# Batch 1's transposes in one run, one more group of block 2 by quarter products, and key-value products in two other PSUM banks: a fused attention and feed-forward kernel on Trainium2

## The chip, the cores and the metric

The kernel runs on one core of a Trainium2 chip. The metric is the device time of one execution in microseconds. The profile used here is one profiled execution; its engines are TensorE (PE in the profile), VectorE (DVE), ScalarE (ACT), GpSimd (POOL) and SyncE (SP). The differences to be read are a few tenths of a per cent.

## What is computed

For 8 batches and 8 heads, 576 tokens of 64 numbers go through a linear attention without softmax, and its normed rows (8 × 576 = 4608 tokens of 512) through a feed-forward pair with a leaky step between:

```python
kv = np.einsum('bhsd,bhse->bhde', k, v)
out = np.einsum('bhsd,bhde->bhse', q, kv)
rms = np.sqrt(np.mean(out * out, axis=-1, keepdims=True) + 1e-06)
x = (out / rms * g_norm)            # then (4608, 512)
h = x @ w_in                        # 512 -> 2048
g = np.maximum(h, 0.0) + alpha * np.minimum(h, 0.0)
return (g @ w_out).astype(np.float32)
```

## The kernel before

The 4608 tokens are worked in nine **blocks** w = 0 to 8 of 512 tokens. A block's life has these steps, and the names in brackets are those of the order described below.

- **Attention.** k, v and q of a batch are loaded by DMAs that POOL issues (`ld`, behind one-element gate copies that hold a load back until a given result is there, L1478). q is transposed, for batches 0 and 1 on PE by `step_t` (L361, matmuls with an identity into a PSUM tile, then a copy into SBUF), later by DMA transposes on SP (`q`, L405). The key-value products (`kv`, in `kv_runs`, L1407 for batches 3 on) are 72 matmuls of 64×64. ACT copies them to SBUF as `kv_masked` (`kvc`, three copies, L1419 and L1422). The row products (`R`, L575) multiply q with them; ACT squares the rows (`q2`, `q3`, L635, one instruction and one read of the accumulator per head), takes the root (`rs`), DVE scales them (`n`, L661), and SP transposes the result into `xt` by DMA (`x`, L673).
- **First product** (`m1`), x by w_in, in four groups s of 4 × 128 hidden features. A plain group (`M`, L695, or `Ma` with `M` in column pieces, L728) is four matmuls of 128×512 into one PSUM bank; ACT makes the negative part (`r`, L704), DVE the leaky step (`s`, L710) into `gt`. From the block given in `M1_FROM` on, a group goes by **quarter products** instead (`f.w.s.n`, L1296): seven products of quarters, four matmuls of 128×256 each, as in Strassen's scheme, so that 28 matmuls of 256 columns stand for 16 of 512. They need sums of quarters of the weights (`a.s.n`, made once) and of x (`t.w.n`, DVE, L1280 to L1286, made once a block), three ACT copies of partial sums (`seed`, `u2`, `u3`, L1312 and L1315), two DVE sums (`c22`, `c12`, L1318), and per result half a step on ACT (L1356) and on DVE (`s11` and so on, L1363).
- **Second product** (`p`, L948), gt by w_out, also by quarter products with sums (`S`) on DVE; for the first block plain (L740, tiles `y`). Results are put together (`y.w…`) and stored (`st`).

PSUM has eight banks. Three (`h0` to `h2`) serve the first product, two more (`m0`, `m1`, pool `psm`) the first product from block 2 on; the row products and the key-value products share a two-bank tile (`row_tile`, pool `psr2`); one holds the second product.

**What sets the order.** Blocks 0 and 1 are written out in program order. From block 2 on a table `ORDER` of 1085 step names gives the order in which steps are issued, on all engines; each step's function `put_…` lists the steps that it needs. `LATE_KV` = 4: key-value products of batches 4 to 7 are put only after the first two norms of the row tile (`first` in the diff), since they take the row tile's banks, and the second row products of that batch wait for their copies.

Of the kernel before, what the change touches and what calls it, by code (L numbers as in the profile page):

```python
# [17 lines left out]
def kernel(  # L18
# [1833 lines left out]
    for w in range(1, NW):  # L1852
# [9 lines left out]
        ld.q.4.1@s.2.2 S.2.3.0 M.2.8 y.1.u3 ld.v.4.1@- M.2.10 q3.3.1 q3.3.0 p.1.4.0 p.1.4.1 rs.3.1
        p.1.4.2 r.2.8 n.3.1 p.2.1.0 rs.3.0 r.2.10 p.1.4.3 n.3.0 x.3.1 r.2.9 p.2.1.1 S.1.4.0 y.1.c21
        R.3.3 s.2.9 p.2.1.2 q2.3.2 x.3.0 a.1.2 p.1.5.0 S.2.3.1 p.1.5.1 q2.3.3 S.1.4.3 p.2.1.3
        S.1.4.2 q3.3.2 p.1.5.2 s.2.10 p.1.5.3 q3.3.3 M.2.11 a.1.4 s.2.8 rs.3.2 M.2.13 rs.3.3 n.3.2
        r.2.11 y.2.p1 n.3.3 M.2.12 x.3.2 r.2.13 s.2.11 M.2.14 r.2.12 S.2.1.0 ld.v.4.0@s.2.11 x.3.3
        p.2.2.0 y.1.c22 R.4.1 s.2.12 M.2.15 q.4.3 q2.4.0 S.2.2.0 p.2.2.1 r.2.14 s.2.13 p.1.3.0 q.4.2
        r.2.15 p.1.3.1 s.2.14 q3.4.0 p.1.3.2 s.2.15 p.1.3.3 q.4.0 q2.4.1 Ma.3.0 S.2.1.1 M.3.1 q3.4.1
        t.3.1 q.4.1 y.1.c12 ld.q.5.1@! rs.4.0 M.3.0 t.3.3 rs.4.1 M.3.2 y.2.seed n.4.1 st.1.c11 r.3.0
        M.3.3 n.4.0 r.3.2 t.3.2 x.4.0 kv.4 s.3.0 r.3.3 r.3.1 p.2.6.0 S.2.2.1 ld.q.5.4@! kvc.4  # L1870
        f.3.1.1 s.3.2 p.2.6.1 ld.v.5.1@s.2.9 a.3.4 p.2.6.2 f.3.1.seed t.3.4 p.2.6.3 S.2.4.1 f.3.1.6
        y.2.u2 s.3.3 ld.q.4.4@s.2.10 R.4.3 f.3.1.u2 p.2.7.0 s.3.1 q.5.3 q2.4.3 ld.k.5.1@! f.3.1.2
        S.2.4.0 f.3.1.7 f.3.1.r11 f.3.1.5 x.4.1 f.3.1.u3 p.2.7.1 ld.q.5.0@! q3.4.3 p.2.2.2 f.3.1.c22
# [6 lines left out]
        f.3.2.s12 q2.5.1 f.3.3.7 f.3.3.5 S.3.1.0 q.5.0 f.3.3.u3 p.2.5.3 q2.5.0 f.3.3.c22 f.3.3.2  # L1880
        f.3.3.4 y.2.c22 q.4.4 f.3.3.r11 f.3.3.3 f.3.3.r21 S.3.2.0 p.2.3.0 q3.5.0 p.2.3.1 f.3.3.c12
        q.5.2 p.3.1.2 f.3.3.s11 f.3.3.r12 p.2.3.2 f.3.3.r22 p.3.1.3 f.3.3.s12 q.5.4
        ld.q.6.0@f.3.3.s11 Ma.4.0 y.3.p1 f.3.3.s22 p.2.3.3 q3.5.1 st.1.c22 st.1.c12 M.4.0 f.3.3.s21
        M.4.2 r.4.0 st.2.c11 rs.5.0 s.4.0 p.3.2.0 rs.5.1 r.4.2 M.4.1 t.4.1 s.4.2 f.4.1.1 r.4.1 t.4.2
# [118 lines left out]
```

## Time and profile before

| | |
|---|---|
| median of 3 runs | 267.34 us (267.1 to 267.72) |
| profiled execution, its own time | 267.1 us |
| its span | 265.3 us |
| PE matmuls | 2709, busy 259.0 us (98%) |
| DVE, ACT, POOL busy | 234.7 (88%), 200.1 (75%), 84.9 (32%) |
| DMA moved | 35.79 MB, mean 135 GB/s |

The span is the profiled part of the execution; the 1.8 us around it are the start and the end. Busy time is the time that an engine's instructions cover, and a PE that is 98% busy need not be at its best pace: what a matmul costs is read from the distance between starts. In rows of the timeline the columns are start, length (us), engine, line, operation, output<-inputs, shape and count; a bracket is the idle time of that engine ahead of the row, and what ended it.

### The profile page before, as it was taken

Reading aid. Unit: us, or ns where it says so; the run is one execution under the profiler, and the core shown is the slowest. Engines: PE = TensorE matmul, PEld = TensorE weight load, DVE = VectorE, ACT = ScalarE, POOL = GpSimd, SP = SyncE. Lnnn points to the kernel's source line nnn. Section 1 sums busy time; section 2 is a strip of 40 time slices with the busy share of each in tenths; the row PEclk is TensorE's granted clock in tenths of the full one; section 3 lists DMA queues with packets and bytes.
Section 4 is the critical chain, followed back from the end, with each engine's and each line's share of the span. In section 5 each row is a group of like instructions: output and inputs, shape, how many; then the busy total and the mean of one; then the engine's idle time right before and its main releaser. Section 6 shows DMA issues by size and latency. Waiting matters only on the chain.

```text
span 265.3 us, 7216 instructions
## 1 busy us (share of the span) xinstructions
PE 259.0 (98%) x2709; PEld 189.7 (71%) x2709; DVE 234.7 (88%) x474; ACT 200.1 (75%) x707; POOL 84.9 (32%) x147
## 2 busy tenths in 40 slices
PE   5999999999999999999999999999999999999995
PEld 2464454456657568886888688878887888788884
DVE  6459955899886998999999999999999999989993
ACT  2567627777569899998899899979988976778400
POOL 8763552363142219044332180810005000015300
PEclk9999999999999999999999999999999999999999
DMA  7999999998968999999999989897404221104223
GB/s 193 188 201 206 196 197 190 193 194 222 129 92 134 143 133 131 151 153 129 187 141 124 158 157 168 153 212 115 58 20 122 41 42 40 42 0 162 79 81 121
DMA packets 65031, 35.79 MB, mean 135 GB/s; under 512 B 37396, under 2 KB 63012, under 8 KB 64996
## 3 DMA queue, kind: packets, MB, share of 16 engines
q0 software_dynamic: 31792, 24.47, 59.7%
q1 hardware_dynamic: 32500, 10.11, 25.7%
q10 hardware_dynamic: 704, 0.75, 0.9%
q8 instruction: 21, 0.34, 0.6%
q14 instruction: 14, 0.11, 0.2%
HBM read 36.71 MB, written 9.44 MB: 174 GB/s over the span
## 4 chain that ended last, share of the span: by engine, by line
PE 95%; DMA 2%; SPq 1%; ACT 0%; DVE 0%; issue 0%
PE h_ps L695 21%; PE yY L948 16%; PE mY L1296 12%; PE yX L948 11%; PE yZ L948 10%; PE mV L1296 6%; PE y L740 5%; PE mX L1296 3%; PE h_ps L728 2%; PE or_ps L575 2%; DMA y_sb<-in_g_norm_dram 2%; PE kv_ps L1407 1%; PE ssq_ps L500 1%; PE ot_ps L477 1%; PE qt_ps L361 1%; PE h_ps L1105 1%
## 5 line engine op out<-in xcount | busy, mean ns | idle before, releaser
L695 PE MATMUL h_ps<-xt,w_in_sb 128*128 128x512 f16 x252 | 59.6, 379 | 0.0
L710 DVE SCALAR_TENSOR_TENSOR gt<-m_sb,beta_sb,h_ps 128x512 f16<-128x512 f32 x72 | 51.4, 740 | 5.1 <-ACT m_sb L704 4.4
L948 PEld LDWEIGHTS <-s 128*128 128x128 f16 x496 | 47.8, 98 | 7.1 <-DVE s L866 0.5
L704 ACT ACTIVATE m_sb<-h_ps 128x512 f32<-128x512 f32 x72 | 41.7, 607 | 14.1 <-PE h_ps L695 9.1
L752 POOL DMA_DIRECT2D out_dram<-y_sb x37 | 21.6, 591 | 72.0 <-ACT y_sb L1004 38.7
L948 PEld LDWEIGHTS <-gt 128*128 128x128 f16 x384 | 37.3, 98 | 7.4
L635 ACT ACTIVATE sq_sb<-or_ps 128x64 f16<-128x64 f32 x192 | 41.0, 269 | 1.0 <-PE or_ps L575 1.0
L695 PEld LDWEIGHTS <-w_in_sb 128*128 128x128 f16 x252 | 24.2, 98 | 24.4 <-issue 0.3
L635 ACT ACTIVATION_READ_ACCUMULATOR sq_sb<-or_ps 128x1 f32 x192 | 40.3, 254 | 0.0
L948 PE MATMUL yX<-w_out_sb,gt 128*128 128x256 f16 x256 | 37.8, 273 | 0.0
L948 PE MATMUL yY<-wsum,s 128*128 128x256 f16 x256 | 34.4, 273 | 0.0
L1363 DVE SCALAR_TENSOR_TENSOR gt<-m_sb,beta_sb,mh 128x256 f16<-128x256 f32 x72 | 30.9, 477 | 0.6 <-ACT m_sb L1356 0.5
L1318 DVE TENSOR_TENSOR mh<-mV,mu 128x512 f32<-128x512 f32 x36 | 24.7, 687 | 3.3 <-PE mV L1296 1.5
L1356 ACT ACTIVATE m_sb<-mh 128x512 f32<-128x512 f32 x36 | 23.1, 647 | 4.4 <-DVE mh L1318 4.0
L1315 ACT COPY mu<-mY 128x512 f32<-128x512 f32 x36 | 21.6, 599 | 4.5 <-PE mY L1296 4.0
L1296 PEld LDWEIGHTS <-w_in_sb 128*128 128x128 f16 x216 | 20.9, 98 | 3.0
L661 DVE TENSOR_TENSOR x_rows<-or_ps,rstd_r 128x512 f16<-128x512 f32 x27 | 18.1, 683 | 3.0 <-ACT rstd_r L645 2.9
L948 PE MATMUL yZ<-wsum,s 128*128 128x256 f16 x120 | 17.2, 273 | 0.0
L948 PE MATMUL yY<-wsum,gt 128*128 128x256 f16 x128 | 16.9, 272 | 0.0
L740 PE MATMUL y<-w_out_sb,gt 128*128 128x512 f16 x64 | 16.3, 380 | 0.0
L212 POOL DMA_DIRECT2D qst<-in_q_dram x12 | 9.5, 791 | 20.1 <-DMA qt_sb<-qst 15.7
L948 PE MATMUL yZ<-w_out_sb,s 128*128 128x256 f16 x120 | 15.9, 273 | 0.0
(161 smaller groups left out, 466.4 us busy)
## 6 DMA issues: line engine op xcount, KB each, us to landing
kst<-in_k_dram POOLq DMA_DIRECT2D x10, 288.0 KB, 6.6
vst<-in_v_dram POOLq DMA_DIRECT2D x10, 288.0 KB, 6.5
qst<-in_q_dram POOLq DMA_DIRECT2D x10, 256.0 KB, 5.1
out_dram<-y_sb POOLq DMA_DIRECT2D x18, 128.0 KB, 4.6
w_out_sb<-in_moe_w_out_dram POOLq DMA_DIRECT2D x8, 256.0 KB, 12.0
out_dram<-y_sb POOLq DMA_DIRECT2D x7, 256.0 KB, 5.1
out_dram<-y_sb SPq DMA_DIRECT2D x5, 256.0 KB, 2.3
w_in_sb<-in_moe_w_in_dram POOLq DMA_DIRECT2D x2, 512.0 KB, 10.0
```

The costliest lines, as they stand in the source:

```text
L635: nc.scalar.activation(out=sq[:, half, j], in_=o_ps[:, half, j], func=AF.Square, accum_out=ssq[:, half, j : j + 1],)
L695: nc.tensor.matmul(out=h_ps[:], lhsT=w_in_blk(c, g), rhs=xts[w][:, c, :], start=(c == 0), stop=(c == NC - 1),)
L704: nc.scalar.activation(out=neg[w, g][:], in_=h_ps[:], func=AF.Relu, scale=-1.0)
L710: nc.vector.scalar_tensor_tensor(out=gts[w, i][:, r, :], in0=neg.pop((w, g))[:], scalar=beta_sb[:, g : g + 1], in1=h_ps[:], op0=ALU.mult, ...
L740: nc.tensor.matmul(out=y[:], lhsT=gt_cols(w, g, a * P, (a + 1) * P), rhs=w_out_blk(g), start=(n == 1), stop=(n == NF),)
L752: engs[store_turn[0] % len(engs)].dma_start(out=dst, in_=src)
L948: nc.tensor.matmul(out=bank, lhsT=lhs, rhs=rhs, start=fresh, stop=(c == NK - 1), skip_group_check=True,)
L1296: nc.tensor.matmul(out=t[bank][:, r, :], lhsT=lhs[:, c, r * P : (r + 1) * P], rhs=rhs[:, c, :], start=(fresh and c == r == 0), stop=(c == ...
L1315: nc.scalar.copy(out=t[what][:], in_=t["Y"][:])
L1318: nc.vector.tensor_add(out=h_tile(t, what)[:], in0=src[:], in1=u[:])
L1356: nc.scalar.activation(out=dst, in_=h, func=AF.Relu, scale=-1.0)
L1363: nc.vector.scalar_tensor_tensor(out=gts[w, i][:, r, cols], in0=m, scalar=beta_sb[:, g : g + 1], in1=h, op0=ALU.mult, op1=ALU.add,)
```

## The change

Four things are done.

1. The four transposes of batch 1's q on PE are issued in one run, before the second product's matmuls with which they were interleaved, with two of their PSUM tiles from another pool (`O_POOL` in place of `S_POOL` and `Q_POOL`); the second half of batch 1's key-value products also goes to `O_POOL`.
2. `M1_FROM[3]` goes from 3 to 2: group 3 of block 2 is made by quarter products. Four plain groups (`M.2.12` to `M.2.15`) go, `f.2.3.…` and `t.2.1` to `t.2.4` come.
3. Key-value products of batches 4 to 7 go into a tile of two banks of the first product (`m0`, `m1`, taken by a new pool `pskv`). They need the earlier users of these banks instead of the row tile's norms, the first product's next use of the banks needs `kvc`, and the row tile waits only for its own norms.
4. `ORDER` is a new table of 1097 names.

```diff
-    step_t(1, 0, S_POOL)
-    step_t(1, 1, Q_POOL, nc.vector.tensor_copy)
+    step_t(1, 0, O_POOL)
+    step_t(1, 1, O_POOL, nc.vector.tensor_copy)
+    step_t(1, 3, Q_POOL)
+    step_t(1, 2, S_POOL, nc.vector.tensor_copy)
     y_run(3, (8,))
-    step_t(1, 3, O_POOL)
     y_run(0, (9,))
-    step_t(1, 2, S_POOL, nc.vector.tensor_copy)
     y_run(3, (9,))
     step_kv(1, 0, O_POOL)
-    step_kv(1, 1, S_POOL)
+    step_kv(1, 1, O_POOL)
...
-    M1_FROM = {1: 3, 2: 3, 3: 3}
+    M1_FROM = {1: 3, 2: 3, 3: 2}
...
+    def open_m(name):
+        m_ctx.close()
+        m_pool[:] = [m_ctx.enter_context(tc.tile_pool(name=name, bufs=1, space=bass.MemoryType.PSUM)), name]
+
+    def kv_tile(shape, name):
+        open_m("pskv")
+        return m_pool[0].tile(shape, FP32, name=name, tag="kv")
...
     def kv_runs(b):
-        kv_tiles[b] = row_tile([2, H, D], "kv_ps")[:, :, 0 : NPAIR // 2, :]
+        if b >= LATE_KV:
+            kv_ps = kv_tile([P, 2, H, D], "kv_ps")
+        else:
+            kv_ps = row_tile([2, H, D], "kv_ps")
+        kv_tiles[b] = kv_ps[:, :, 0 : NPAIR // 2, :]
...
     def put_m1(w):
+        if LATE_KV <= w + 1 < B:
+            kv_old[w + 1] = bank_free["m0"] + bank_free["m1"]
+            bank_free["m0"] = bank_free["m1"] = (("kvc", w + 1),)
...
-            first = (("n", w, 0), ("n", w, 1)) if w >= LATE_KV else ()
-            step(("kv", w), "kv", lambda: kv_mm(w), (*loaded, *free, *first))
+            step(("kv", w), "kv", lambda: kv_mm(w), (*loaded, *(kv_old[w] if w >= LATE_KV else free)))
...
-            free = (("kvc", w),) if LATE_KV <= w < B else tuple(("n", w, i) for i in tiles)
+            free = tuple(("n", w, i) for i in tiles)
...
-        kv.3 Ma.2.0 kvc.3 S.1.1.3 M.2.3 S.1.1.2 S.1.1.1 y.1.seed M.2.0 a.2.2 M.2.1 S.1.1.0 S.1.2.1
+        y.1.seed kv.3 M.2.1 S.1.1.1 t.2.1 p.1.2.3 r.2.1 M.2.3 S.1.1.2 S.1.1.0 a.1.1 Ma.2.0 r.2.3
```

**Where instructions stand, on PE.** First, batch 1's q in the middle of the second product of block 0. Before (`qst` is q as loaded, `qt_ps` its transpose, `y_…` the output tiles):

```order
L740 MATMUL y_579<-w_out_sb_176,gt 128x512
L361 LDWEIGHTS qst
L361 MATMUL qt_ps<-ident_202,qst 64x128
...
L740 MATMUL y_576<-w_out_sb_176,gt 128x512
L361 LDWEIGHTS qst
...
L740 MATMUL y_577<-w_out_sb_176,gt 128x512
L361 LDWEIGHTS qst
...
L740 MATMUL y_576<-w_out_sb_176,gt 128x512
L458 LDWEIGHTS kst
```

The same place of the changed kernel (L374 is the old L361, L754 the old L740, L471 the old L458):

```order
L754 MATMUL y_579<-w_out_sb_176,gt 128x512
L374 LDWEIGHTS qst
L374 MATMUL qt_ps<-ident_202,qst 64x128
...
L754 MATMUL y_576<-w_out_sb_176,gt 128x512
L754 MATMUL y_577<-w_out_sb_176,gt 128x512
L754 MATMUL y_576<-w_out_sb_176,gt 128x512
L471 LDWEIGHTS kst
```

All 32 transposes now stand together, and the three output matmuls behind them.

Second, the key-value products of batch 4 (`kst`, `vst`). Before, they stand between a plain group of block 3 and the second product of block 2:

```order
L695 MATMUL h_ps<-xt,w_in_sb_166 128x512
L1407 LDWEIGHTS kst
L1407 MATMUL kv_ps<-vst,kst 64x64
L948 LDWEIGHTS s_1621
L948 MATMUL yY<-wsum_624,s_1621 128x256
```

In the changed kernel (L588 is the old L575, L1425 the old L1407, L962 the old L948, L1310 the old L1296):

```order
L588 LDWEIGHTS qt_sb_120
L588 MATMUL or_ps<-kv_masked,qt_sb_120 128x64
L1425 LDWEIGHTS kst
L1425 MATMUL kv_ps<-vst,kst 64x64
L1310 LDWEIGHTS vst
L1310 MATMUL mV<-xt,vst 128x256
```

They moved to directly behind batch 4's first row products, among the quarter products of block 2. Batch 6's have moved likewise behind `R.6.1`; batches 5 and 7 still stand between large matmuls.

Third, what follows batch 5's products in the changed kernel (L742 is the old L728, L709 the old L695):

```order
L1425 MATMUL kv_ps<-vst,kst 64x64
L962 LDWEIGHTS s_1991
L962 MATMUL yZ<-w_out_sb_188,s_1991 128x256
L742 LDWEIGHTS w_in_sb_157
L742 MATMUL h_ps<-xt,w_in_sb_157 128x384
L742 MATMUL h_ps<-xt,w_in_sb_157 128x128
L709 LDWEIGHTS w_in_sb_166
L709 MATMUL h_ps<-xt,w_in_sb_166 128x512
```

Before, batch 5's products stood inside block 4's quarter products; now block 4's first groups follow them, and the 128x512 group in the last row is the first that takes one of the two banks in which the products lie.

More of the change, by code (lines that the diff above doesn't have):

```diff
@@ L73 @@
     m_pool = []
+    m_ctx = ExitStack()
     def late_pools():
@@ L79, in late_pools, with m_tile @@
         ]
-        m_pool.append(
-            ctx.enter_context(tc.tile_pool(name="psm", bufs=1, space=bass.MemoryType.PSUM))
-        )
+        ctx.enter_context(m_ctx)
+        open_m("psm")
+    def open_m(name):
+        m_ctx.close()
+        m_pool[:] = [m_ctx.enter_context(tc.tile_pool(name=name, bufs=1, space=bass.MemoryType.PSUM)), name]
+    def m_tile(shape, name, tag):
+        if m_pool[1] != "psm":
+            open_m("psm")
+        return m_pool[0].tile(shape, FP32, name=name, tag=tag)
+    def kv_tile(shape, name):
+        open_m("pskv")
+        return m_pool[0].tile(shape, FP32, name=name, tag="kv")
     def row_tile(shape, name):
@@ L689, in m1_bank @@
     def m1_bank(tag, shape, name):
-        pool = ps_h if tag[0] == "h" else m_pool[0]
-        return pool.tile(shape, FP32, name=name, tag=tag)
+        if tag[0] == "m":
+            return m_tile(shape, name, tag)
+        return ps_h.tile(shape, FP32, name=name, tag=tag)
     def m1_mm(h_ps, w, g, cs):
@@ L1862 @@
[L1862 to L1873, printed above, removed]
@@ L1880 @@
[L1880 to L1884, printed above, removed]
-        p.3.2.1 y.2.c12 f.4.1.seed M.4.3 s.4.1 y.3.seed f.4.1.6 t.4.4 f.4.1.2 t.4.3 f.4.1.u2 S.3.1.1
@@ new lines @@
+        S.2.3.1 q3.3.2 M.2.11 S.1.4.3 a.1.3 q3.3.3 f.2.3.2 t.2.4 f.2.3.6 y.1.c22 rs.3.2 p.2.1.2
+        r.2.11 n.3.2 f.2.3.5 f.2.3.u2 s.2.11 p.1.3.0 x.3.2 rs.3.3 f.2.3.r11 f.2.3.7 n.3.3 p.2.1.3
+        f.2.3.u3 f.2.3.s11 p.1.3.1 x.3.3 y.2.p1 f.2.3.4 f.2.3.c22 p.1.3.2 ld.q.5.4@f.2.3.s11
+        f.2.3.r21 S.2.1.0 q.4.1 R.4.1 f.2.3.r22 kv.4 f.2.3.s21 q2.4.0 f.2.3.3 S.2.2.0 q.4.0 p.1.3.3
+        kvc.4 p.2.2.0 f.2.3.c12 p.2.2.1 f.2.3.s22 q.4.2 f.2.3.r12 Ma.3.0 q3.4.0 y.1.c12 M.3.0
+        ld.k.5.1@f.2.3.s22 M.3.2 f.2.3.s12 q.4.3 y.2.seed M.3.1 r.3.0 t.3.1 rs.4.0 S.2.1.1
@@ L1955 @@
+        p.8.5.3 p.8.4.0 y.8.c22 p.8.4.1 p.8.4.2 p.8.4.3 p.8.3.0 y.8.c21 p.8.3.1
     """.split()
```

172 lines of the change are left out of this document (93 added, 79 removed).

## The prediction

> **What bounds the kernel now.** I read the busy shares first, then the waits, then stage windows, then single rows of the timeline.
>
> ```profile
> PE 259.0 (98%) x2709; PEld 189.7 (71%) x2709; DVE 234.7 (88%) x474; ACT 200.1 (75%) x707; POOL 84.9 (32%) x147
> PEclk9999999999999999999999999999999999999999
> PE 95%; DMA 2%; SPq 1%; ACT 0%; DVE 0%; issue 0%
> ```
>
> TensorE (PE) is busy for 259.0 of 265.3 us, the granted clock shows no loss in any slice, and 95% of the chain that ended last is PE. The table of PE's waits says what the rest is (total, times, longest):
>
> ```profile
> PE warm_ps L324 <- DVE y_sb L133: 1.5, 1, 1.5
> PE alpha_ps L1069 <- DMA y_sb<-in_g_norm_dram: 0.9, 1, 0.9
> PE qt_ps L361 <- DVE qst L1059: 0.4, 1, 0.4
> ```
>
> All three belong to the start, before any edited code. From there PE runs through, so only two things move the end: PE's own work, and a wait that the new order brings. The windows of blocks 2, 3 and 4 (length, then busy PE, PEld, DVE, ACT, POOL with counts) show how near other engines stand:
>
> ```profile
> 66.60:94.60 28.00, 28.00 (x307) 18.39 (x305) 23.53 (x45) 21.80 (x116) 6.69 (x15) 1.00 0.91 124
> 94.60:120.00 25.40, 25.40 (x310) 20.82 (x309) 24.35 (x50) 24.42 (x106) 10.30 (x19) 1.00 1.13 144
> 120.00:147.70 27.70, 27.70 (x337) 22.93 (x336) 26.54 (x55) 25.34 (x112) 8.86 (x16) 1.00 1.13 142
> ```
>
> PE has no gap; VectorE (DVE) has 4.47 us free in block 2's window and about 1.1 in the two after it.
>
> **Part 1, batch 1's transposes in one go.** PE's timeline before:
>
> ```profile
> 36.10 0.64 PE L361 MATMUL qt_ps<-ident,qst 128*64 128x128 f16 x16
> 36.67 0.39 PE L740 MATMUL y<-w_out_sb,gt 128*128 128x512 f16 x1
> 36.98 0.41 PE L361 MATMUL qt_ps<-ident,qst 128*64 128x128 f16 x8
> 37.33 0.39 PE L740 MATMUL y<-w_out_sb,gt 128*128 128x512 f16 x1
> ...
> 38.32 0.32 PE L458 MATMUL kv_ps<-vst,kst 128*64 128x64 f16 x8
> ```
>
> One output matmul and eight transposes take 37.33 − 36.67 = 0.66 us. Without a change of shape they would take 0.216 (a 512-column matmul, priced below) plus some 0.22 for the transposes (sixteen take 36.67 − 36.10 = 0.57 with one change, so eight take about half of the 0.45 that is left). So one round trip between the shapes costs about 0.225. The stretch from the first transpose to the key-value products is 2.22 us; it holds three trips into the transposes, one of which stays: **−0.45**. The bounds are −0.45 and 0: nothing is gained if the chain behind the transposes (copies of q, then batch 1's rows) is what PE would meet next. The trace has no wait there, so I take −0.45. The copies into SBUF now come in one bunch, with three matmuls and the key-value products as cover.
>
> **Part 2, four groups of block 2 as quarter products.** The pitches come from the chain of waits, which counts runs of equal matmuls:
>
> ```profile
> 85.01 0.87 PE yZ L948 x8
> 87.20 3.45 PE h_ps L695 x16
> ```
>
> A 512-column matmul costs 3.45/16 = 215.7 ns, a 256-column one 0.87/8 = 109 ns. Removed are 16 of the first (3.45 us), added 28 of the second (3.05): **−0.40**. By these rows two halves cost only 2 × 109 − 215.7 = 2.3 ns more than a whole. The Trainium skill ("TensorEngine Tiling (Array Packing)", section "Instruction Overhead") gives every matmul some 60 cycles of overhead, which speaks against cutting matmuls in halves: 16 × (512 + 60) against 28 × (256 + 60) is a saving of 3.3%, 0.11 us instead of 0.40, and the whole sum would be −0.6. The two rows above differ from that by far, and I go by the rows.
>
> What the other engines do for it (count, then busy us and mean ns, from the groups by form):
>
> ```profile
> L710 DVE SCALAR_TENSOR_TENSOR gt<-m_sb,beta_sb,h_ps 128x512 f16<-128x512 f32 x72 | 51.4, 740 | 5.1 <-ACT m_sb L704 4.4
> L1363 DVE SCALAR_TENSOR_TENSOR gt<-m_sb,beta_sb,mh 128x256 f16<-128x256 f32 x72 | 30.9, 477 | 0.6 <-ACT m_sb L1356 0.5
> L1318 DVE TENSOR_TENSOR mh<-mV,mu 128x512 f32<-128x512 f32 x36 | 24.7, 687 | 3.3 <-PE mV L1296 1.5 <-ACT mu L1315 1.2
> L1280 DVE TENSOR_TENSOR t<-xt 128x512 f16<-128x512 f16 x6 | 2.5, 415 | 0.0
> 82.53 1.37 DVE L661 TENSOR_TENSOR x_rows<-or_ps,rstd_r 128x512 f16<-128x512 f32 x2 [2.30 <-ACT rstd_r L645]
> ```
>
> Four sums of x, two of products and eight half-width evacuations come, four full ones go: 4 × 0.415 + 2 × 0.687 + 8 × 0.475 − 4 × 0.740 = +3.9 us of DVE by durations, about 3.1 by start-to-start distance, since neighbours overlap. Block 2's 4.47 free microseconds cover that, so I cost it at **nothing**. The largest piece of that room is the 2.30 in the last row, where DVE waits for ScalarE (ACT) in batch 3's norms. If the new order leaves it idle, 2.2 us of room are left for 3.1 us of work, and PE waits about 0.9. ACT gets some 1.6 us more and has 6.2 free.
>
> **Part 3, key-value products in two banks of the first product.** Two things change on PE. First, where they stand: batches 4 and 6 now come directly behind the row products of the same batch, whose shape is small too. Before, each stood between large matmuls:
>
> ```profile
> 54.23 0.20 PE L1389 MATMUL kv_ps<-vsb,ksb 128*64 128x64 f16 x2
> 54.36 0.29 PE L575 MATMUL or_ps<-kv_masked,qt_sb 64*128 64x64 f16 x8
> ...
> 128.07 0.60 PE L948 MATMUL yX<-w_out_sb,gt 128*128 128x256 f16 x4
> 128.60 0.78 PE L1407 MATMUL kv_ps<-vst,kst 64*64 64x64 f16 x72
> 129.31 0.61 PE L1296 MATMUL mV<-xt,spare 128*128 128x256 f16 x4
> ```
>
> Batch 5's entry costs 0.53 − 4 × 0.109 = 0.09 us beyond the four matmuls. A change between two small shapes (54.23 to 54.36, of which the two products hide little) costs up to 0.12. So a merged pair saves between 0 and 0.21; I take the entry, nearest to what is removed, twice: **−0.19**, with 0 and −0.42 as ends.
>
> Second, the banks: the first product of the next block may use them again only when ACT has copied the products out. Batch 3 shows how long that takes:
>
> ```profile
> 66.78 0.80 PE L1407 MATMUL kv_ps<-vst,kst 64*64 64x64 f16 x72
> 67.52 0.82 PE L728 MATMUL h_ps<-xt,w_in_sb 128*128 128x384 f16 x4
> 67.83 0.37 ACT L1419 CAST kv_masked<-kv_ps 128x256 f16<-128x256 f32 x1 [1.21 <-PE kv_ps L1407]
> 68.21 0.74 ACT L1422 CAST kv_masked<-kv_ps 64x256 f16<-64x256 f32 x2
> ```
>
> The copies end at 68.95, 1.43 us after PE has gone on at 67.52. For batch 5 the new order puts on PE four second-product matmuls (0.44), 4 × 384 columns (0.65) and 4 × 128 (0.22) between the products and the first group in such a bank: 1.30 of cover, so a wait of 0.13; with ACT a little late I take **+0.15**. Queued behind it on PE is all of block 4's first product. Behind batch 7 stand 12 × 0.109 + 4 × 128 columns (0.22) = 1.53, behind batch 4 about 1.75, behind batch 6 far more: nothing. Upper end: ACT comes to the copies a half pass of squares late, which is
>
> ```profile
> 155.19 0.23 ACT L635 ACTIVATE sq_sb<-or_ps 128x64 f16<-128x64 f32 x1
> ...
> 155.97 0.62 ACT L1315 COPY mu<-mY 128x512 f32<-128x512 f32 x1
> ```
>
> 0.78 us for four heads, so up to 0.93 for batch 5. The row tile's second half no longer waits for these copies; PE did not wait there, so that earns nothing.
>
> **Part 4, the loads.** The products move about 6, 9, 10 and 4 us earlier on PE, counted by its work ahead of them. For batch 5 they go from 128.6 to about 119, so its k and v must land by then:
>
> ```profile
> 104.83 9.33 SPq L673 DMA_TRANSPOSE xt<-x_rows  x3
> 112.69 0.18 POOL L1478 COPY gate_sb<-xt 1x1 f16<-1x1 f16 x1 [7.16 <-DMA xt<-x_rows]
> 115.50 0.72 POOL L202 DMA_DIRECT2D vst<-in_v_dram  x1
> vst<-in_v_dram POOLq DMA_DIRECT2D x10, 288.0 KB, 6.5
> ```
>
> Before, GpSimd's (POOL's) last load for it leaves at 115.50, after a gate on transposed x that POOL waited 7.16 us for, and lands 6.5 later, at 122.0. In the new order that gate's transpose is no longer behind batch 4's other half and a transpose of batch 5's q on SP, so I expect the issue near 108 and landing near 115: **nothing**. If the gate stays at 112.7, PE waits 122.0 − 119 = 3 us.
>
> The other steps of the new order trade places within their block: PE's work in them is unchanged, and stores, q's transposes and weight sums keep the same counts on POOL, SP and DVE. I cost them at nothing, under the cover that PE has no row of waiting there now; where that cover fails it is DVE or ACT that is late, which rivals (a) and (c) price.
>
> **The sum.** −0.45 − 0.40 − 0.19 + 0.15 = −0.89. On the profiled execution's own 267.1 us (span 265.3) that gives 266.2; that execution is 0.24 below the median of 267.34, so against the median it is **266.4**. The terms' lower ends together (−0.45, −0.40, −0.42, 0) are −1.27, or 266.1; the largest single step upward, 0.9 us, whether DVE's or a late copy's, gives 267.3. The three runs before lie within 0.3 us of their middle one, and with that on both sides the range is 265.8 to 267.6.
>
> **Rivals.** (a) DVE binds in block 2, as priced: −0.89 + 0.9 = 0, 267.3. For it: the room is in pieces between ACT's results. Against: block 3's window already holds quarter products at 24.35 of 25.40 without a gap of PE. (b) The transposes' gain is lost behind them, 266.4 + 0.45 = 266.85. (c) Slower: ACT reaches the copies late at batches 4, 5 and 7, and PE stops before the first product. With a lag L the waits are L − 0.32, L + 0.13 and L − 0.10; against −1.04 for the rest, the gain is gone at L = 0.44 and a loss of 0.2% stands at L = 0.62. At one half pass of squares, 0.78, they add up to 2.05 and give 267.34 − 1.04 + 2.05 = 268.35. For it: ACT is busy 24.42 of 25.40 us in block 3, and squares stand ahead of the copies of batches 4 and 5. Against: these squares are released by products that PE ends before or during the key-value run. (d) Batch 5's loads stay late: 266.4 + 3 = 269.4. (e) The merges save their upper end and batch 5 has no wait: 267.34 − 1.27 = 266.1.
>
> **How the numbers follow.** Forecast 0.60; (a) 0.11; (b) 0.08; (c) 0.10; (d) 0.04; (e) 0.07. A measurement of this kernel can tell about 0.2%, 0.53 us, from no change: faster is below 266.8. Faster are the forecast and (e): 0.67; same are (a) and most of (b): 0.19; slower are (c) and (d): 0.14. The range 265.8 to 267.6 leaves out (c), (d) and a little of (a).
>
> **What would show it.** In the changed kernel's profile: sixteen output matmuls and transposes in batch 1 without alternation, the stretch near 1.77 us; PE's table of waits still with three rows, or one small row on batch 5's copies; the stretch of the quarter products of block 2 without a gap; key-value products starting within 0.1 us of the row products at batches 4 and 6. A row of PE waiting for ACT's copies, for DVE's sums in block 2, or for k and v would make the prediction wrong, in that order of likelihood; so would DVE gone from its 4.47 us of room to none.

## The result and the profile after

The changed kernel is **slower**: 269.0 us in the median of 20 runs (267.72 to 274.77) against 267.27 for the kernel before (266.95 to 268.42). The ratio is 1.0059, with a 95% interval of 1.0040 to 1.0079. Ratios here leave out executions more than 1.5% above the fastest of their kernel (of the changed kernel's 20 those of 272.43, 272.73 and 274.77), medians do not, and the profiles of e3 and e7 are of such executions. The forecast was 266.4, with a range up to 267.6. The profiled execution took 268.11 us, with a span of 266.3.

The page of the changed kernel, busy shares:

```profile
PE 258.5 (97%) x2721; PEld 191.3 (72%) x2721; DVE 237.3 (89%) x484; ACT 202.6 (76%) x710; POOL 87.8 (33%) x154
```

PE is busy 0.5 us less than before, and the span is 1.0 us longer. The table of PE's waits has a row that the old one lacks (its other two are those of the start):

```profile
PE or_ps L588 <- DMA qt_sb<-qsb: 1.1, 1, 1.1
```

`or_ps` are the row products, `qt_sb<-qsb` the DMA transpose of the rest tokens of a batch's q (q.3.4 in the order). The timeline of SP, before:

```profile
70.14 3.45 SPq L405 DMA_TRANSPOSE qt_sb<-qst  x2
73.77 1.17 SPq L405 DMA_TRANSPOSE qt_sb<-qsb  x1
75.05 2.51 SPq L405 DMA_TRANSPOSE qt_sb<-qst  x2
```

and after:

```profile
70.07 4.76 SPq L418 DMA_TRANSPOSE qt_sb<-qst  x3
74.93 1.20 SPq L418 DMA_TRANSPOSE qt_sb<-qsb  x1
76.22 1.22 SPq L418 DMA_TRANSPOSE qt_sb<-qst  x1
```

The new order puts three transposes of q ahead of q.3.4 in place of two, so it is issued 1.16 us later. The view of that single instruction gives its landing time, before:

```profile
DMA to landing us min/median/max: 2.3/2.3/2.3
```

and after:

```profile
DMA to landing us min/median/max: 3.9/3.9/3.9
```

It landed at 73.77 + 2.3 = 76.1 before and at 74.93 + 3.9 = 78.8 after. It is needed behind the first 8 of the 24 products of batch 3's first rows (R.3.1). PE before, where all 24 run through:

```profile
77.81 0.56 PE L575 MATMUL or_ps<-kv_masked,qt_sb 64*64 64x64 f16 x24
```

and after, where PE reaches them 0.3 us earlier:

```profile
77.48 0.31 PE L588 MATMUL or_ps<-kv_masked,qt_sb 64*64 64x64 f16 x8
78.84 0.54 PE L588 MATMUL or_ps<-kv_masked,qt_sb 64*64 64x64 f16 x16 [1.05 <-DMA qt_sb<-qsb]
```

The eight products ahead take some 0.12, so the sixteen were due at 77.9 before. So 1.9 us of slack, which no view of before had named because nothing waited there, became a wait. The place on SP is not the whole of it: had q.3.4 landed in 2.3 us again, it would have been there at 77.2. e16, the same kernel in a later profile, has it in the same place, and there it lands at 76.3 (2.3 us) and nothing waits. What goes with it is how soon POOL's load of batch 4's q follows it. After, and in e16:

```profile
75.33 0.76 POOL L225 DMA_DIRECT2D qst<-in_q_dram  x1 [3.89 <-DMA qt_sb<-qst]
```

```profile
74.02 1.20 SPq L418 DMA_TRANSPOSE qt_sb<-qsb  x1
...
75.05 0.76 POOL L225 DMA_DIRECT2D qst<-in_q_dram  x1 [3.34 <-DMA qt_sb<-qst]
```

The load is issued 0.40 us behind q.3.4 in the first and 1.03 behind it in e16. All profiles that give q.3.4's landing fall in line: 2.3 us in the eight with the load 0.9 us or more behind it (before, e4, e12 to e14, e16 to e18), 3.7 to 4.4 in the seven with 0.4 to 0.6 (after, e2, e5, e9 to e11, e15), and 6.1 in e3, where the load stands 1.0 ahead of it. No run moves this load alone, so it is a regularity of the profiles and not a shown cause.

The other places, each with its row. Batch 1's transposes:

```profile
36.25 1.08 PE L374 MATMUL qt_ps<-ident,qst 128*64 128x128 f16 x32
37.27 0.82 PE L754 MATMUL y<-w_out_sb,gt 128*128 128x512 f16 x3
38.02 0.32 PE L471 MATMUL kv_ps<-vst,kst 128*64 128x64 f16 x8
```

38.02 − 36.25 = 1.77 us, as forecast. The merged key-value products of batch 4, and those of batch 5 with what follows:

```profile
92.92 0.41 PE L588 MATMUL or_ps<-kv_masked,qt_sb 64*128 64x64 f16 x16
93.26 0.90 PE L1425 MATMUL kv_ps<-vst,kst 64*64 64x64 f16 x72
94.09 0.61 PE L1310 MATMUL mV<-xt,vst 128*128 128x256 f16 x4
...
120.42 0.89 PE L1425 MATMUL kv_ps<-vst,kst 64*64 64x64 f16 x72
121.24 0.61 PE L962 MATMUL yZ<-w_out_sb,s 128*128 128x256 f16 x4
121.69 1.04 PE L742 MATMUL h_ps<-xt,w_in_sb 128*128 128x384 f16 x8
122.56 0.59 PE L709 MATMUL h_ps<-xt,w_in_sb 128*128 128x512 f16 x2
```

No wait for the copies behind batch 5 (121.69 to 122.56 is 0.65 + 0.22 for eight column pieces), none for its loads, and none on DVE in block 2. And the last matmuls, before and after (the spans are 265.3 and 266.3):

```profile
260.95 1.06 PE L943 MATMUL yZ<-w_out_sb,s 128*128 128x128 f16 x16
```

```profile
261.33 1.06 PE L957 MATMUL yZ<-w_out_sb,s 128*128 128x128 f16 x16
```

From that row to the end of the span it is 4.4 us before and 5.0 after. This is the whole account of the 1.0 us. With batch 3's key-value products as a mark (66.78 before, 66.44 after): the first transpose comes 0.15 later; from it to the mark it is 30.68 before and 30.19 after, −0.49; from the mark to the last matmuls 194.17 and 194.89, +0.72; the end +0.6. The +0.72 hold the stop at R.3.1 (1.24 us: the sixteen products start 1.36 after the eight ahead of them, whose own time is some 0.12), so everything else in that stretch is 0.5 **shorter**.

### The profile page after: what moved, and what is told of

It reads as the page before. It is cut to its first block, busy times and chain, and to the rows that moved or that the text cites. A ratio compares the mean times of both kernels' runs of the same rounds, so it can differ in the third digit from the quotient of the medians.

```text
span 266.3 us, 7277 instructions
## 1 busy us (share of the span) xinstructions
PE 258.5 (97%) x2721; PEld 191.3 (72%) x2721; DVE 237.3 (89%) x484; ACT 202.6 (76%) x710; POOL 87.8 (33%) x154
## 4 chain that ended last, share of the span: by engine, by line
PE 94%; DMA 3%; SPq 1%; ACT 0%; DVE 0%; issue 0%
PE h_ps L709 19%; PE yY L962 15%; PE mY L1310 13%; PE yX L962 11%; PE yZ L962 10%; PE mV L1310 6%; PE y L754 5%; PE mX L1310 3%; PE h_ps L742 2%; PE or_ps L588 2%; DMA y_sb<-in_g_norm_dram 2%; PE kv_ps L1425 1%; DMA qt_sb<-qsb 1%; PE ssq_ps L513 1%; PE ot_ps L490 1%; PE qt_ps L374 1%
## 5 line engine op out<-in xcount | busy, mean ns | idle before, releaser
L709 PE MATMUL h_ps<-xt,w_in_sb 128*128 128x512 f16 x236 | 56.8, 379 | 0.0
L962 PEld LDWEIGHTS <-s 128*128 128x128 f16 x496 | 48.1, 98 | 7.3 <-DVE s L880 0.2
L724 DVE SCALAR_TENSOR_TENSOR gt<-m_sb,beta_sb,h_ps 128x512 f16<-128x512 f32 x68 | 48.8, 742 | 4.5 <-ACT m_sb L718 3.7
L718 ACT ACTIVATE m_sb<-h_ps 128x512 f32<-128x512 f32 x68 | 39.8, 608 | 11.3 <-PE h_ps L709 8.5
L962 PEld LDWEIGHTS <-gt 128*128 128x128 f16 x384 | 37.3, 98 | 7.2
L709 PEld LDWEIGHTS <-w_in_sb 128*128 128x128 f16 x236 | 22.4, 98 | 21.7 <-issue 0.3
L962 PE MATMUL yX<-w_out_sb,gt 128*128 128x256 f16 x256 | 36.6, 273 | 0.0
L962 PE MATMUL yY<-wsum,s 128*128 128x256 f16 x256 | 34.3, 273 | 0.0
L1377 DVE SCALAR_TENSOR_TENSOR gt<-m_sb,beta_sb,mh 128x256 f16<-128x256 f32 x76 | 32.9, 478 | 0.6 <-ACT m_sb L1370 0.6
L1370 ACT ACTIVATE m_sb<-mh 128x512 f32<-128x512 f32 x38 | 24.8, 652 | 5.2 <-DVE mh L1332 5.1
L1332 DVE TENSOR_TENSOR mh<-mV,mu 128x512 f32<-128x512 f32 x38 | 26.0, 685 | 1.8 <-ACT mu L1329 1.2
L1329 ACT COPY mu<-mY 128x512 f32<-128x512 f32 x38 | 23.0, 604 | 4.8 <-PE mY L1310 4.5
L1496 POOL COPY gate_sb<-gt 1x1 f16<-1x1 f16 x21 | 7.0, 332 | 54.0 <-DVE gt L1377 38.5
L1310 PEld LDWEIGHTS <-w_in_sb 128*128 128x128 f16 x228 | 22.1, 98 | 3.3
L1377 DVE SCALAR_TENSOR_TENSOR gt<-m_sb,beta_sb,mY 128x256 f16<-128x256 f32 x38 | 16.4, 473 | 0.2
L1377 DVE SCALAR_TENSOR_TENSOR gt<-m_sb,beta_sb,mX 128x256 f16<-128x256 f32 x38 | 16.4, 473 | 0.0
L962 PE MATMUL yZ<-wsum,s 128*128 128x256 f16 x120 | 16.1, 273 | 0.0
L962 PE MATMUL yZ<-w_out_sb,s 128*128 128x256 f16 x120 | 16.1, 273 | 0.0
```

Of the source, the lines that this page charges most:

```text
L709: nc.tensor.matmul(out=h_ps[:], lhsT=w_in_blk(c, g), rhs=xts[w][:, c, :], start=(c == 0), stop=(c == NC - 1),)
L718: nc.scalar.activation(out=neg[w, g][:], in_=h_ps[:], func=AF.Relu, scale=-1.0)
L724: nc.vector.scalar_tensor_tensor(out=gts[w, i][:, r, :], in0=neg.pop((w, g))[:], scalar=beta_sb[:, g : g + 1], in1=h_ps[:], op0=ALU.mult, ...
L962: nc.tensor.matmul(out=bank, lhsT=lhs, rhs=rhs, start=fresh, stop=(c == NK - 1), skip_group_check=True,)
L1310: nc.tensor.matmul(out=t[bank][:, r, :], lhsT=lhs[:, c, r * P : (r + 1) * P], rhs=rhs[:, c, :], start=(fresh and c == r == 0), stop=(c == ...
L1329: nc.scalar.copy(out=t[what][:], in_=t["Y"][:])
```

## The experiments

**e1 to e4, one chip: is it the place of q.3.4 on SP?** e1 is the changed kernel with one swap, e2 the changed kernel again, e3 the kernel before with the same swap the other way, e4 the kernel before with part 1 alone (its diff is the first piece of the change).

```diff
 # e1, in ORDER of the changed kernel
-        p.1.6.0 r.2.5 S.1.2.2 p.1.6.1 q.3.2 y.1.c11 t.2.2 M.2.6 a.1.2 s.2.0 p.1.6.2 q.3.4
+        p.1.6.0 r.2.5 S.1.2.2 p.1.6.1 q.3.4 y.1.c11 t.2.2 M.2.6 a.1.2 s.2.0 p.1.6.2 q.3.2
 # e3, in ORDER of the kernel before: q.3.4 and q.3.2 change places
-        s.2.2 p.1.6.2 p.1.6.3 s.2.0 q.3.4 M.2.6 s.2.1 M.2.4 r.2.6 q.3.3 ld.q.4.0@s.2.2 y.1.u2 s.2.6
+        s.2.2 p.1.6.2 p.1.6.3 s.2.0 q.3.2 M.2.6 s.2.1 M.2.4 r.2.6 q.3.3 ld.q.4.0@s.2.2 y.1.u2 s.2.6
```

> The changed kernel with one swap in the order: the transpose of batch 3's rest tokens (q.3.4) goes to SP third, as before, and q.3.2 fourth. Theory A (the loss is one wait: batch 3's first row products wait for q.3.4, which stands behind one more transpose on SP): the row of PE waiting for qt_sb from qsb, 1.1 us, is gone, the other three rows stay, the span falls by about 1.1, and the median lies near the forecast, 266.3 to 267.0, with a spread as small as that of the kernel before. Rival B (the loss of the median over the profiled run, and its spread of several microseconds, come from another place, such as batch 5's loads or the copies of the key-value products): the row goes, but the median stays above 267.5 and the spread stays.

> The changed kernel once more, unedited, for a second profile. Theory A: the same single new row of PE waiting for qt_sb from qsb, between 0.5 and 4 us, and the time of the profiled run over 267.0 equals it within 0.3. Rival B: a second new row, or a time that this row does not account for.

> The kernel before with the same swap the other way: q.3.4 goes to SP behind all four other transposes of batch 3's q, in place of third. Theory A: it is issued near 76.2 in place of 73.8, lands 2.3 to 3.9 us later, at 78.5 to 80.1, and the first row products need it at 77.9, so PE gets a row of 0.6 to 2.2 us and the kernel is slower by that: 267.9 to 269.5. Rival B (the landing is set by the load and the DMA engines, not by the place in SP's queue): no change, 267.3.

> The kernel before with part 1 of the change alone, batch 1's transposes in one run. Prediction's step: 0.45 us less, 266.85, ratio 0.9983. Rival (the chain behind the transposes takes it back, or it only moves block 2's wait): 267.3.

e3 is the plain one. PE's timeline there:

```profile
77.81 0.31 PE L575 MATMUL or_ps<-kv_masked,qt_sb 64*64 64x64 f16 x8
82.64 0.75 PE L575 MATMUL or_ps<-kv_masked,qt_sb 64*64 64x64 f16 x16 [4.52 <-DMA qt_sb<-qsb]
```

The swap alone costs the kernel before 1.5% (ratio 1.0152, 1.0095 to 1.0208; median 273.06). So the place in SP's queue is enough to bring the wait, which was twice the upper end of what theory A expected. The chain of e3's profile shows why it was so long:

```profile
76.46 6.14 DMA qt_sb<-qsb
```

The later issue alone, with a landing of 2.3, would have made PE wait until 78.8; the other 3.8 us are the longer landing. A long stop also costs more than itself. Stretches of e3's profile behind it (the third number from the end is the granted clock of TensorE, 1.00 in all of these stretches before):

```profile
84.00:86.00 2.00, 2.00 (x7) 0.84 (x6) 0.00 (x0) 2.00 (x19) 0.00 (x0) 0.50 1.32 201
88.00:90.00 2.00, 2.00 (x20) 1.72 (x18) 1.82 (x4) 1.30 (x4) 0.00 (x0) 1.00 0.31 62
```

The granted clock is 0.50 from 82 to 86 us and 0.78 from 86 to 88, and the twelve 512-column matmuls there take 3.90 us in place of 12 × 0.2157 = 2.59. From the mark to the last matmuls e3 takes 200.87, 6.70 more than before: 4.7 of stop and 2.0 behind it. e7 has the same behind its stop of 3.5 us (clock 0.56 and 0.59 in the four us from 72). Behind the stops of 1.1 to 1.8 us in the changed kernel, e1 and e15 the clock stays at 1.00.

e1 removed the wait at R.3.1 as expected, but not the loss (1.0004, 0.9974 to 1.0034; 267.97 in the median). Its lowest time, 266.23, is just the forecast on the profiled run, and its highest 270.96. The unedited kernel on the same chip (e2) is no slower (1.0007), so the ratios cannot tell what the swap is worth. e1's profiled execution took 269.39, with these rows:

```profile
84.03 0.35 PE L588 MATMUL or_ps<-kv_masked,qt_sb 64*128 64x64 f16 x12
84.86 0.23 PE L588 MATMUL or_ps<-kv_masked,qt_sb 64*128 64x64 f16 x4 [0.47 <-DMA qt_sb<-qst]
...
102.52 0.35 PE L588 MATMUL or_ps<-kv_masked,qt_sb 64*128 64x64 f16 x12
104.45 0.23 PE L588 MATMUL or_ps<-kv_masked,qt_sb 64*128 64x64 f16 x4 [1.58 <-DMA qt_sb<-qst]
```

Batch 3's second products (R.3.3) waited for the last transpose of q.3, and batch 4's second products (R.4.3) for that of q.4. e2, the unedited kernel, waits 0.7 us for `qsb` at 77 and 0.9 for `qst` at 102 (1.0007, 0.9975 to 1.0039). So theory A, one wait at one place, was too narrow: R.3.1 and R.4.3 are weak in the new order, and the waits differ from run to run. e4 gave 0.9989 (0.9966 to 1.0011), 267.14: in its profiled execution the stretch to the mark is 30.25, so the 0.4 us are there, and 0.9 us of a wait for q at R.3.3 in the kernel before's own order.

**e5 to e8, one chip: earlier loads and earlier transposes.**

```diff
 # e5: load q of batch 3 earlier
-    LOADS = {(1, 1): (("k", 3), ("v", 3)), (1, 13): (("q", 3),)}
+    LOADS = {(1, 1): (("k", 3), ("v", 3)), (1, 11): (("q", 3),)}
 # e6: q.4.0 and q.4.1 taken from beside R.4.1 to ahead of x.3.2
-        r.2.11 n.3.2 f.2.3.5 f.2.3.u2 s.2.11 p.1.3.0 x.3.2 rs.3.3 f.2.3.r11 f.2.3.7 n.3.3 p.2.1.3
+        r.2.11 n.3.2 f.2.3.5 f.2.3.u2 s.2.11 p.1.3.0 q.4.0 q.4.1 x.3.2 rs.3.3 f.2.3.r11 f.2.3.7 n.3.3 p.2.1.3
 # e7: both, in the changed kernel; e8: both, in the kernel before
```

> The changed kernel with batch 3's q loaded two units of block 1 earlier, some 1.7 us; nothing else. Theory A2 (the loss is PE's waits for DMA transposes of q, which land 2.3 to 8 us after their issue, at the two row products that the new order leaves without slack: batch 3's first, for q.3.4, and batch 4's second, for q.4.3): the transposes of q.3 start near 68.4 in place of 70.1, the wait at 77 us is gone, the one near 102 us stays (0 to 1.7 us): 0.7 to 1.2 us less than the changed kernel. Rival B2 (waits of one place only hand their time to the next one, because the DMA queues are what lags): the time is that of the changed kernel, with longer waits near 84 and 102 us.

> The changed kernel with the transposes q.4.0 and q.4.1 put on SP ahead of x.3.2, into the 3 us in which SP waits for that row's norm; nothing else. A2: q.4.2 and q.4.3 are issued 2 to 3 us earlier, land before 101, and the wait near 102 us is gone; the one at 77 us (0.7 to 1.2) stays, so 0 to 1 us less than the changed kernel. B2: the x transposes behind them come later, and PE waits for x.3.2 or x.3.3 in block 3's first product instead.

> Both edits of q in the changed kernel. A2: no row of PE waiting for qt_sb; PE's rest is the prediction's sum without the wait, so 266.3 to 266.6 against 267.3 of the kernel before: ratio 0.996 to 0.9975. B2: 267.5 to 268.5, with a wait elsewhere.

> The same two edits of q in the kernel before. A2: the kernel before had 1 to 2 us of slack at these places in its profiled run, so little is gained: 267.0 to 267.3, with a narrower spread; e7 is then 0.8 below it (the prediction's parts 1 and 2). B2: the same as the kernel before, and e7 not below it.

e5 is 1.1% slower than the kernel before (1.0113, 1.0064 to 1.0163), more than the changed kernel in any of its three sets of runs (1.0007 to 1.0059). The wait at 77 went, as A2 said. But the earlier load runs beside the transposes of x for block 2, and PE waits there:

```profile
66.22 0.69 PE L1425 MATMUL kv_ps<-vst,kst 64*64 64x64 f16 x64
68.15 1.02 PE L709 MATMUL h_ps<-xt,w_in_sb 128*128 128x512 f16 x4 [1.23 <-DMA xt<-x_rows]
```

The landing of those transposes, in the changed kernel and in e5:

```profile
DMA to landing us min/median/max: 2.4/2.5/4.9
```

```profile
DMA to landing us min/median/max: 4.0/5.6/7.2
```

With 1.8 us for `qst` at 102 beside it, more was lost than gained: rival B2 was right that waits move on, though it had not named this one. e7 (median 272.75, no ratio to be had) and e8 (1.0021, 0.9983 to 1.0059) carry the same load and the same row on `xt`, 3.5 and 1.3 us, so they tell nothing about the change. (e17, without this load, waits there for 1.0 us too, so the load is not the only thing that brings this wait.) e6 did what A2 said: the wait at 102 went, the one at 77 stayed (the other two rows of its table are those of the start):

```profile
PE or_ps L588 <- DMA qt_sb<-qsb: 0.8, 1, 0.8
```

It stands even with the kernel before (0.9999, 0.9968 to 1.0031; 267.72).

**e9 to e12, one chip: a later need, and the parts one by one.** e9 is e6 with R.3.1 and its squares moved behind one plain group and four products of the second product. The others are e9 with one part of the change undone: the first piece of the diff (e10), the merged places of kv.4 and kv.6 (e11), block 2's quarter products (e12).

```diff
 # e9
-        p.1.7.1 p.1.7.2 r.2.6 ld.v.4.0@s.2.0 M.2.9 r.2.4 s.2.6 S.1.4.0 R.3.1 r.2.9 s.2.4
-        ld.k.4.0@s.2.1 M.2.10 q2.3.0 a.2.2 a.3.4 p.1.7.3 q2.3.1 t.2.3 M.2.7 a.2.4 ld.v.4.1@- y.1.u3
+        p.1.7.1 p.1.7.2 r.2.6 ld.v.4.0@s.2.0 M.2.9 r.2.4 s.2.6 S.1.4.0 r.2.9 s.2.4
+        ld.k.4.0@s.2.1 M.2.10 a.2.2 a.3.4 p.1.7.3 t.2.3 R.3.1 M.2.7 q2.3.0 q2.3.1 a.2.4 ld.v.4.1@- y.1.u3
 # e11
-        f.2.3.r21 S.2.1.0 R.4.1 f.2.3.r22 kv.4 f.2.3.s21 q2.4.0 f.2.3.3 S.2.2.0 p.1.3.3
+        f.2.3.r21 S.2.1.0 R.4.1 f.2.3.r22 f.2.3.s21 q2.4.0 f.2.3.3 kv.4 S.2.2.0 p.1.3.3
-        f.4.2.s22 x.5.3 R.6.1 f.4.3.u3 kv.6 q2.6.1 S.4.3.0 p.4.1.0 y.3.c22 q.6.3 p.4.1.1 q3.6.1
+        f.4.2.s22 x.5.3 R.6.1 f.4.3.u3 q2.6.1 S.4.3.0 p.4.1.0 kv.6 y.3.c22 q.6.3 p.4.1.1 q3.6.1
 # e12: and in ORDER the names of f.2.3 give way to M.2.12 to M.2.15 with r and s, all ahead of kv.4; t.2.1 to t.2.4 go
-    M1_FROM = {1: 3, 2: 3, 3: 2}
+    M1_FROM = {1: 3, 2: 3, 3: 3}
```

> The changed kernel with q.4.0 and q.4.1 ahead of x.3.2 on SP (as in e6), and batch 3's first row products R.3.1 put one plain group and four second-product matmuls later on PE, 1.3 us, with their squares behind them; no load and no transpose of q.3 is moved. Theory A3 (the change's own terms are as predicted and its only loss is PE reaching R.3.1 and R.4.3 before their q has landed; what helps is a later need, since the DMA engines are full and an earlier load only delays other transposes): no row of PE waiting for qt_sb in the profile, profiled run and lowest time 266.2 to 266.6, median 0.5 to 1 below the kernel before's. Rival B3 (the waits wander: with these gone, the later norms of batch 3 or the loads of batch 4 are late): a row of 0.5 us or more elsewhere, median not below the kernel before's.

> e9 with part 1 undone: batch 1's transposes interleaved with the output matmuls as before. Prediction's step: 0.45 us more than e9. Rival (the gain of part 1 is lost at batch 2's row products or key-value products, whose k, v and q land when they land): 0 to 0.2 more, with rows of PE waiting near 52 us in e9 that are smaller here.

> e9 with key-value products of batches 4 and 6 each put behind the next large matmuls (four quarter matmuls, or four second-product matmuls), so that they stand alone again. The prediction's step: 0.19 us more. Theory C (products directly behind row products pay a change in and a change within, as the profile of the changed kernel shows at 93.14 and 93.78 us): 0 to 0.06 more.

> e9 with part 2 undone: the last four groups of block 2 are plain again, and the sums of x of block 2 go. Prediction's step: 0.40 us more PE work, 266.7 to 267.0. Rival: no more, because DVE's 3 us in block 2 cost PE as much as the quarter products save, or less, because row products come later by it and their q has then landed.

e9 falls on B3's side (1.0029, 1.0012 to 1.0045). Its profile still has 0.5 us for `qsb`, and two new rows of 0.5 us:

```profile
82.92 1.91 PE L962 MATMUL yY<-wsum,gt 128*128 128x256 f16 x16 [0.52 <-ACT u L1010]
...
86.17 0.41 PE L588 MATMUL or_ps<-kv_masked,qt_sb 64*128 64x64 f16 x16 [0.47 <-DVE x_rows L674]
```

With the squares later, ACT is late for a copy of the second product, and DVE is late with the norms that free the row tile for R.3.3. R.3.1 is held on both sides. The comparison of the parts still holds, since e10 to e12 share these two stops; the one for `qsb` is e9's alone. From the first transpose to the mark e10 takes 30.69 and e9 30.20: part 1 is worth 0.49. From the mark to the last matmuls e12 takes 196.06 and e9 195.68; taking out each one's idle time of PE in that stretch (0.53, 0.48 and, ahead of kv.4, 0.39 in e12; 0.47, 0.52 and 0.47 in e9) leaves 194.66 and 194.22, so part 2 is worth about 0.45. For the merge, e9's and e11's rows at batch 4:

```profile
94.10 0.41 PE L588 MATMUL or_ps<-kv_masked,qt_sb 64*128 64x64 f16 x16
94.44 0.91 PE L1425 MATMUL kv_ps<-vst,kst 64*64 64x64 f16 x72
95.28 0.61 PE L1310 MATMUL mV<-xt,vst 128*128 128x256 f16 x4
95.72 0.60 PE L962 MATMUL yZ<-w_out_sb,s 128*128 128x256 f16 x4
```

```profile
94.05 0.41 PE L588 MATMUL or_ps<-kv_masked,qt_sb 64*128 64x64 f16 x16
94.39 0.61 PE L1310 MATMUL mV<-xt,vst 128*128 128x256 f16 x4
94.94 0.78 PE L1425 MATMUL kv_ps<-vst,kst 64*64 64x64 f16 x72
95.64 0.61 PE L962 MATMUL yZ<-w_out_sb,s 128*128 128x256 f16 x4
```

The same work takes 95.72 − 94.10 = 1.62 us merged and 95.64 − 94.05 = 1.59 apart. The same stretch at batch 6, through its eight 256-column matmuls, takes 2.03 and 2.04. The merge saves nothing, as theory C said: directly behind row products the 72 products take 0.84 us, alone 0.70. The three medians, 268.72, 268.62 and 269.47 against e9's 268.54, are too widely spread to add to this.

**e13 to e16, one chip: both cures, with transposes moved only.** e13 is e1 and e6 together. e14 and e15 move batch 4's v loads later, e14 on top of e13, e15 alone. e16 is the changed kernel again.

```diff
 # e14 and e15: ld.v.4.0 and ld.v.4.1 leave their places and follow batch 4's last q, without a gate
-        S.1.4.2 M.2.8 S.2.3.0 q3.3.1 a.1.4 q3.3.0 p.1.4.0 ld.q.4.1@s.2.4 p.1.4.1 rs.3.1 p.1.4.2
+        S.1.4.2 M.2.8 S.2.3.0 q3.3.1 a.1.4 q3.3.0 p.1.4.0 ld.q.4.1@s.2.4 ld.v.4.0@! ld.v.4.1@! p.1.4.1 rs.3.1 p.1.4.2
```

> The changed kernel with both cures that move transposes only: q.3.4 third on SP (e1) and q.4.0, q.4.1 ahead of x.3.2 (e6). Row products, loads and PE's order are the changed kernel's own. Theory A4 (the loss is the waits of PE for transposed q at R.3.1 and R.4.3, and transposes land late when loads run beside them): the waits at 77 and 102 us are gone, one at R.3.3 near 84 us of 0 to 0.7 is left (two transposes are issued after 75.5, beside the four loads of batch 4's k and v), median 266.6 to 267.1, lowest 266.2. Rival B4 (the waits wander, e9): median as the unedited changed kernel's on this chip.

> e13 with the two loads of batch 4's v issued behind the last half of batch 4's q, near 83 us in place of 77 and 80, as late as before the change; they are needed at 93. A4: the two last transposes of q.3, which took 7.8 us beside these loads in e1, land by 82, no row of PE waiting for qt_sb: 266.2 to 266.6. B4, or a rival in which the loads do not matter: the wait near 84 stays as in e13, or the products of batch 4 wait for v near 93 us.

> The changed kernel with the two loads of batch 4's v alone issued later, as in e14. If the loads beside them make the transposes land late at R.3.1, its wait (0.8 to 1.2 us) shrinks by half or more; if the place of q.3.4 on SP does it alone (it is issued at 74.9, before these loads in either case), the wait stays, and so does the one near 102 us.

> The changed kernel unedited on the same chip as e13 to e15, for their comparison. A4: rows of PE waiting for qt_sb at 77 us (0.7 to 1.3) and, in some profiles, near 102 us (0 to 1); median 0.5 to 1.5 over e14's.

e13's table of waits is the shortest of all:

```profile
PE warm_ps L337 <- DVE y_sb L146: 1.5, 1, 1.5
PE alpha_ps L1083 <- DMA y_sb<-in_g_norm_dram: 0.6, 1, 0.6
```

On the chip where the unedited kernel (e16) stood at 1.0031 (1.0007 to 1.0055, median 268.36, up to 274.1), e13 stands at 0.9985 (0.9964 to 1.0006, median 267.12, up to 268.25). That is 1.2 us of the median and most of the spread, for three transposes moved on SP. So the places of these transposes on SP make most of the loss. That they do it through PE's waits for q is read from the profiles with such waits (the first one and e2); e16's own profile, 267.31, has only 0.3 us of it. What e13 does not reach is the forecast. e14 (1.0042, 1.0014 to 1.0070) and e15 (1.0030, 1.0006 to 1.0054) do not help: v loaded later lands late itself, e14 waiting 0.6 for `vst` and 0.6 for `xt`, and in e15 the wait at 102 stays, 1.8 us. At 77 neither e15's table nor that of the unedited e16 has a row, and q.3.4 landed in 3.7 us in e15 and in 2.3 in e16, so the earlier loads of v are not what stretches it.

**e17 and e18, one chip: the last 0.5 us.** e13 has no wait left, and from the mark to the last matmuls it takes 260.89 − 67.44 = 193.45, 0.7 less than before. It still ends late:

```profile
67.44 0.78 PE L1425 MATMUL kv_ps<-vst,kst 64*64 64x64 f16 x72
...
260.89 1.06 PE L957 MATMUL yZ<-w_out_sb,s 128*128 128x128 f16 x16
```

With a span of 265.8 that is 4.9 us of end, against 4.4 before.

```diff
 # e17, on e13, in last_block
-            y_sb = ysb_p.tile([P, 2, HC], FP32, name="y_sb")
+            if h == 0:
+                y_piece = ysb_p.tile([P, P], FP32, name="y_last", bufs=1)[:]
+            else:
+                y_piece = ysb_p.tile([P, 2, HC], FP32, name="y_sb")[:, 1, half]
 # e18, the kernel before: q.4.0 and q.4.1 ahead of x.3.2, as in e6
```

> e13 with the first half of the last 128x256 output piece in a tile of its own, so that the DVE addition that makes it no longer waits for two earlier stores and an ACT copy of the output ring beside the last matmuls. In all profiles of the new order the span ends 4.0 to 4.1 us after the last matmul's start, in those of the old order 3.5 to 3.6, and the last but one store is issued at 0.55 in place of 0.33. Theory T (that ring wait costs the 0.5): the tail is 3.5 to 3.7, the store leaves at 0.33, and the time is 0.4 below e13's: 266.6 in the middle, ratio 0.996 to 0.998. Rival (the two last stores contend in the DMA engines whatever the wait): the tail stays at 4.0, time as e13's, 267.1.

> The kernel before with the cure of e6 alone: q.4.0 and q.4.1 ahead of x.3.2 on SP. If what e13 and e17 gain belongs to the change and not to the cure, this one is as the kernel before, 267.0 to 267.5, since its second row products of batch 4 had 2 us of slack; if the cure itself is worth something, it is 0.3 or more below.

Theory T falls. The end of e17:

```profile
260.84 1.06 PE L957 MATMUL yZ<-w_out_sb,s 128*128 128x128 f16 x16
260.89 0.96 ACTq L766 DMA_DIRECT2D out_dram<-y_sb  x2
...
261.49 0.29 DVE L1744 TENSOR_TENSOR y_last<-yZ,u 128x128 f32<-128x128 f32 x1
262.23 0.35 ACTq L766 DMA_DIRECT2D out_dram<-y_last  x1
```

The addition into the tile of its own (`y_last`) is done at 261.78, but ACT issues its store only at 262.23, though its store before ended at 261.85. The end is 265.8 − 260.84 = 5.0 as in e13. So the ring is not it, and what ACT does in between stays open. e17's ratio is 0.9993 (0.9974 to 1.0013, median 267.59; its profiled execution waited 1.0 us for `xt` in block 2). e18 is the kernel before, 0.9998 (0.9973 to 1.0024, 267.35): the cure by itself gives it nothing. In its profile the transposes of x that now stand behind q's come late, and PE waits 1.0 us for one at 96, as B2 had feared for e6. No version here beats the kernel before beyond its interval; e13 is the nearest.

## Why the prediction was wrong

**Where it failed** is the paragraph on the other steps of the new order: "I cost them at nothing, under the cover that PE has no row of waiting there now". A table of waits shows where slack is below zero, not how much there is above it. The queue of transposes on SP was looked at for x and for the gate of batch 5's loads, and not for q. The rows for it were there: q.3.4 landed at 76.1 for products at 77.9, 1.9 us of slack, while the new order issues it one transpose (1.2 us) later and PE comes 0.3 us earlier. That alone left 0.4, and a landing of 3.9 in place of 2.3 turned it into the 1.24 us of stop. That a landing is no constant was on view too: the profile before has landings of 2.3 to 6.9 us for the transposes of q.3. The price was 0.3 to 1.6 us of waits for q in the profiles of the changed kernel (1.1; 0.7 and 0.9; 0.3). e3 and e13, which move only transposes on SP, show from both sides that their order is the cause.

**Part 1**, −0.45: right; −0.49 in the changed kernel and between e10 and e9. Rival (b) is not what happened, although e4 shows waits at other places taking it back.

**Part 2**, −0.40: right, about −0.45 (e12 against e9). The two-halves price of the rows held. Rival (a) did not come: from 66.40 to 94.20 PE is busy for 26.75 of 27.80 us, and the 1.05 left are the wait at R.3.1.

**Part 3**, −0.19 for the merges: wrong. I priced the entry as if the key-value products behind row products needed none; e9 against e11 gives 0.03 the other way at batch 4 and nothing at batch 6. The Trainium skill (TensorEngine Tiling (Array Packing), section "Key Properties") says that a change of tiling mode, not just of tile, drains TensorE. The rows agree that a change costs time, 0.09 to 0.12 us, and show that the products behind row products (`64*64` behind `64*128` in the rows) pay for one too, 0.84 − 0.70 = 0.14. The wait for the copies, +0.15, did not come in the changed kernel's profile; rival (c) with it. Its bank change alone was not tried.

**Part 4**, loads for batch 5: right, no wait at 120: v's last load leaves POOL at 109.58 and lands at most 6.4 us later, at 116.0. Rival (d) did not come.

**The sum**: in e13, without waits, PE needs 0.49 + 0.72 = 1.2 less than the kernel before from the first transpose to the last matmuls, more than the −0.9 forecast; parts 1 and 2 are 0.94 of it, and the other 0.3 is not assigned. Of that 0.5 goes at the end (4.8 to 5.3 us in every profile of the new order, 4.4 in those of the old), which was costed at nothing too; its cause stays open. In e13's profile the start ate the rest: the first transpose comes at 37.24 in place of 36.10, a time that lies between 35.8 and 37.4 over the profiles. Why the median lies 0.9 above the profiled execution was not seen in a profile of such a run. The three longest executions of the changed kernel (272.43, 272.73 and 274.77) have a mean granted clock of 0.994, 0.994 and 0.987, all others 0.997 or more; e7's profiled execution has 0.992 and e3's 0.986. So stops of 3.5 us or more with a stretch of lowered clock behind them are likely there, and e13's narrower spread fits that, but it is not shown.

## What to carry to other kernels

Before a new order is priced, write down for each transfer that the critical engine consumes when it lands and when it is first needed, and subtract what the new order moves on either side; the table of waits lists only those that are already negative. Compare the queue that issues the transfers (here SP) row by row as carefully as the engine that waits. A cure that starts a load earlier can cost more than it saves (e5). Changing the order among transfers already there is no safer by itself: three transposes moved won back 1.2 us of the median (e13), two exchanged cost 1.5% (e3). And keep stops of the critical engine short: the one of 4.5 us cost 2.0 more in clock.
